# The value weights' loads moved to ScalarE's queue, and three value products moved ahead of the second tile's transposes

## The chip, the cores and the metric

One NeuronCore of a Trainium2 chip runs the whole program. The metric is the device time of one execution in microseconds; the kernel before takes 689.46 us (median of 3 runs, 689.43 to 689.73).

Five engines work side by side and each takes its own instructions in the order in which they were written: PE (TensorE, matmuls; its weight loads are shown as PEld), DVE (VectorE), ACT (ScalarE), POOL (GpSimd) and SP (SyncE, which here only issues transfers). They wait for each other, and for transfers, on semaphores.

## What is computed

A transformer layer with attention and a gated feed-forward side by side, in float32, for 2048 tokens of width 448, 16 heads of 28:

```python
xn = _layernorm(x, axis=-1)
q, k, v = xn @ wq, xn @ wk, xn @ wv            # heads of 28, 4 segments of 512 tokens
for s in range(4):
    p = softmax(qs @ ks.T * scale + mask)
    o = g * (phi(qs) @ M) / (phi(qs) @ z) + (1 - g) * (p @ vs)
    M, z = M + phi(ks).T @ vs, z + phi(ks).sum(0)
h = sigmoid(xn @ w_gate) * (xn @ w_up)
return x + o @ wo + h @ w_down
```

(Shortened from the reference; phi(t) is t+1 above zero and exp(t) below.) The change touches only the start: the normalisation of the first 512 tokens and their product with `wv`.

## The kernel before

**Precision.** Every matmul operand is split in two, a rounded high part and a low remainder, and a product is the sum of high·high, high·low and low·high. The width 448 is held in four chunks of 128 rows, the fourth holding the last 64 rows twice, so one product takes 11 matmuls. `EARLY[0]` (L52) is their order for the first two tiles: n = 0 to 2 use high parts alone (weights `wv[0..2]`), n = 3 to 5 use the low parts of x, n = 6 the fourth chunk, n = 7 to 9 the low parts of the weights (`wv[4..6]`), n = 10 the fourth chunk with `wv[7]`.

**Stages.** For each of four blocks of 512 tokens (four tiles of 128), the front normalises the rows, turns them with PE transposes, and multiplies by the value weights and then by the query/key weights (`keys_queries`, L355). Behind the front come feed-forward and attention, interleaved by a fixed plan (L785 to L794), then the output projection. PE, ACT and DVE take the front's instructions exactly as the code lists them (`FRONT`, L56); POOL's and SP's places are chosen by the scheduler.

**Start of the front (L407 to L494).** SP issues the loads. `acc[0]` receives the rows of x: tile 0 (L409), tile 1 (L410), tiles 2 and 3 in one load (L413). `raw[0]` and `raw[1]` receive the two halves of the value weights, two chunks each (L411, L412). `stage` receives four of seven query/key weight chunks in two loads (L415, L416); the rest goes to `wqk_raw` (L420, L423); `acc[1]` is the next block of x (L421); four small loads fetch the gates (L426).

Hardware transfers signal their end on eight semaphores, here called lanes 0 to 7, which the framework hands out in turn in the order in which the loads are written. A lane that comes up again is used only after its earlier load has landed: the issuing instruction waits for that.

For each tile t: `statistics` (DVE, L294 to L296), `root` (ACT, one Sqrt, L301), `normalised` (DVE reciprocal and scaling, L308 to L320; ACT copies the last 64 columns, L324), `turn_high` (four PE transposes, L95; ACT evicts the high part, L97), `turn_low` (DVE forms the low part, L102 and L103). `split_v(t)` splits chunk t of the value weights: ACT rounds it (L431), POOL subtracts (L432). `value_terms` issues the products (L335), `store_values` evicts them (ACT, L339). `fill(n)` issues n matmuls of the identity with itself whose result nobody reads; `WARM` of them (L442) stand at the very start. `gate_n` (L428) is a dummy Sqrt on ACT that brings the function table in early; the table load stands ahead of it.

Of the kernel before, what the change touches and what calls it, by code (L numbers as in the profile page):

```python
# [17 lines left out]
D = 448  # L18
# [33 lines left out]
EARLY = [HIGH + LOW_X + [(3, 3)] + LOW_W + [(3, 7)], HIGH + LOW_W + LOW_X + [(3, 3), (3, 7)]]  # L52
# [9 lines left out]
def kernel(  # L62
# [10 lines left out]
    nc = tc.nc  # L73
# [17 lines left out]
    def transpose_high(pt, src, dst, t):  # L91

        tok = slice(t * P, (t + 1) * P)
        for c in range(4):
            T.transpose(pt[:, c * P:(c + 1) * P], src[:, c * P:(c + 1) * P], ident)  # L95
        p3 = pt.rearrange("p (c n) -> p c n", c=4)
        A.activation(dst[:, 0:4, tok], p3, AF.Copy)  # L97
        return p3

    def transpose_low(p3, dst, t):  # L100
        tok = slice(t * P, (t + 1) * P)
        V.tensor_sub(dst[:, 4:7, tok], p3[:, 0:3], dst[:, 0:3, tok].bitcast(F32))  # L102
        V.tensor_sub(dst[64:, 3, tok], p3[64:, 3], dst[64:, 3, tok].bitcast(F32))  # L103
# [11 lines left out]
    def bank(name, tag):  # L115
        return ps.tile([P, L], F32, name=name, tag=tag, bufs=banks[tag])
# [32 lines left out]
    def four_k(dtype, name):  # L149
        return mid.tile([P, 2, L], dtype, name=name, tag="4k", bufs=4)  # L150
# [125 lines left out]
    with tc.tile_pool(name="front", bufs=2) as sb, tc.manual_schedule(engines=FRONT):  # L276
# [11 lines left out]
        def statistics(b, t0, steps):  # L288

            stats = sb.tile([P, steps, 6], F32, name=f"stats{steps}")  # L290
            mv = sb.tile([P, steps, 2], F32, name=f"mv{steps}")
            vh = sb.tile([P, steps], F32, name=f"vh{steps}")
            for t in range(steps):
                V.bn_stats(stats[:, t, :], acc[b][:, t0 + t, :])  # L294
                V.bn_aggr(mv[:, t, :], stats[:, t, :])
            V.tensor_scalar(vh, mv[:, :, 1], EPS, -0.5, op0=ALU.add, op1=ALU.mult)  # L296
            return mv, vh

        def root(vh):
            y = sb.tile([P, vh.shape[1]], F32, name=f"y{vh.shape[1]}")  # L300
            A.activation(y, vh, AF.Sqrt, scale=-2.0)  # L301
            return y

        def rstd(mv, vh, y):

            steps = vh.shape[1]
            tm = sb.tile([P, steps], F32, name=f"tm{steps}")
            V.reciprocal(y, y)  # L308
            if steps == 1:
                V.tensor_scalar(tm, y, y, vh, op0=ALU.mult, op1=ALU.mult)  # L310
                V.tensor_scalar(y, tm, 1.5, y, op0=ALU.add, op1=ALU.mult)
            else:
                V.tensor_mul(tm, y, y)
                V.tensor_mul(tm, tm, vh)
                V.scalar_tensor_tensor(y, tm, 1.5, y, op0=ALU.add, op1=ALU.mult)
            return [(mv[:, t, 0:1], y[:, t:t + 1]) for t in range(steps)]

        def normalise(b, t, mean, y):
            xn = sb.tile([P, 512], F32, name="xn")
            V.tensor_scalar(xn[:, :D].rearrange("p (m h c) -> p h m c", h=H, c=4),  # L320
                              acc[b][:, t, :].rearrange("p (h m c) -> p h m c", h=H, c=4), mean, y,
                              op0=ALU.subtract, op1=ALU.mult)
            if b == 0:
                A.activation(xn[:, D:], xn[:, 384:D], AF.Copy)  # L324
            else:
                G.tensor_copy(xn[:, D:], xn[:, 384:D])
            return xn
# [4 lines left out]
        def value_terms(b, t, pv, terms, n0=0, n1=len(TERMS)):  # L332
            for n in range(n0, n1):
                a, w = terms[n]
                T.matmul(pv[:, :D], xs[b][:, a, t * P:(t + 1) * P], wv[w],  # L335
                         start=n == 0, stop=n == len(TERMS) - 1)

        def store_values(b, t, pv):
            A.activation(vst[:, t, :, :DH], pv[:, :D].rearrange("p (h d) -> p h d", d=DH), AF.Copy)  # L339
            if t == NT - 1:  # L340
                nc.sync.dma_start(vd[b], vst.rearrange("p t h d -> p t (h d)"))
# [65 lines left out]
        raw = [four_k(F32, "wv_raw") for _ in range(2)]  # L407
        raw = [r.rearrange("p a n -> p (a n)")[:, :2 * D] for r in raw]
        nc.sync.dma_start(acc[0][:, 0, :], x[0:P, :])  # L409
        nc.sync.dma_start(acc[0][:, 1, :], x[P:2 * P, :])  # L410
        nc.sync.dma_start(raw[0], w_v[:, :2 * D])  # L411
        nc.sync.dma_start(raw[1], w_v[:, 2 * D:])  # L412
        nc.sync.dma_start(acc[0][:, 2:4, :], x[2 * P:L, :].rearrange("(t p) d -> p t d", p=P))  # L413
        raw = [raw[t // 2][:, t % 2 * D:(t % 2 + 1) * D] for t in range(4)]
        nc.sync.dma_start(stage[:, 0:2, :], w_qk[0:2].rearrange("c p n -> p c n"))  # L415
        nc.sync.dma_start(stage[:, 2:4, :], w_qk[2:4].rearrange("c p n -> p c n"))  # L416
        raw_qk = [stage[:, c, :] for c in range(4)]
# [8 lines left out]
                nc.sync.dma_start(gate[32 * j:32 * j + 32], beta[j::HG].partition_broadcast(32))  # L426
        G.memset(vst[:, :, :, DH:], 1.0)
        A.activation(gate_n, vst[:, 0, :NG, DH], AF.Sqrt)  # L428

        def split_v(t):  # L430
            A.activation(wv[t], raw[t], AF.Copy)  # L431
            G.tensor_sub(wv[4 + t], raw[t], wv[t].bitcast(F32))  # L432
# [10 lines left out]
        def fill(n):  # L443
            for _ in range(n):
                T.matmul(warm[:, :P], ident, ident, start=True, stop=True)

        def turn_high(t):
            p3[t] = transpose_high(bank("pt", "s"), xn[t], xs[0], t)

        def turn_low(t):  # L450
            transpose_low(p3[t], xs[0], t)

        def normalised(t):
            xn[t] = normalise(0, t, *rstd(*st[t], y[t])[0])
# [2 lines left out]
        st[0] = statistics(0, 0, 1)  # L457
        y[0] = root(st[0][1])
        normalised(0)
        st[1] = statistics(0, 1, 1)  # L460
        y[1] = root(st[1][1])
        turn_high(0)
        fill(5)
        split_v(0)
        split_v(1)
        normalised(1)
        split_v(2)
        split_v(3)
        turn_low(0)
        turn_high(1)  # L470
        st[2] = statistics(0, 2, 1)
        y[2] = root(st[2][1])
        turn_low(1)
        normalised(2)
        st[3] = statistics(0, 3, 1)
        pv = [bank("pv", "p") for _ in range(2)]
        for t in range(2):
            value_terms(0, t, pv[t], EARLY[0], 0, 7)
        value_terms(0, 0, pv[0], EARLY[0], 7)
        store_values(0, 0, pv[0])  # L480
        y[3] = root(st[3][1])
        turn_high(2)
        value_terms(0, 1, pv[1], EARLY[0], 7)
        store_values(0, 1, pv[1])
# [3 lines left out]
        pv = bank("pv", "p")  # L488
# [345 lines left out]
```

## Time and profile before

| what | value |
|---|---|
| median of 3 runs | 689.46 us |
| the profiled execution, its own time | 689.46 us |
| its span, first to last instruction | 687.7 us |
| PE busy | 681.7 us (99%) |
| DVE busy | 567.4 us (83%) |
| ACT busy | 342.6 us (50%) |
| POOL busy | 151.3 us (22%) |
| transfers | 84.37 MB, mean 123 GB/s |

A row of the timeline gives the start in us, the length, the engine, the line, the operation, what it writes and reads, how many instructions were merged, and in brackets the engine's idle time before it with what ended it. SPq is SyncE's queue; its rows are issues of transfers, not the transfers themselves. A row of the waits gives who waited, for what, us in total, how often, and the longest. A row of the transfers gives what is loaded from where, the number of issues and the size of one.

### The profile page before, as it was taken

How to read it: one execution, taken by the hardware profiler on the slowest of the kernel's cores; microseconds unless marked ns; L12 is line 12 of the kernel's file. 1: busy time of each engine (PE TensorE's matmuls, PEld its weight loads, DVE VectorE, ACT ScalarE, POOL GpSimd, SP SyncE). 2: the span in 40 equal slices, each digit the busy share in tenths (PEclk: the TensorE clock that was granted, in tenths of full speed). 3: DMA queues.
4: the chain of work that ended last, by engine and by line, in shares of the span. 5: the costliest groups of instructions: out<-in, count | busy, mean ns of one | idle time of the engine just before them, and what ended most of it. 6: DMA issues, size and time to landing. Idle time of an engine off the chain costs nothing.

```text
span 687.7 us, 10438 instructions
## 1 busy us (share of the span) xinstructions
PE 681.7 (99%) x3594; PEld 566.6 (82%) x3594; DVE 567.4 (83%) x994; ACT 342.6 (50%) x563; POOL 151.3 (22%) x349
## 2 busy tenths in 40 slices
PE   8999999999999999999999999999999999999997
PEld 7898888778878787787878878787787878878897
DVE  6765795767788988998898989989898899889863
ACT  4837555343554555543655446454653565446320
POOL 3500020101223222232332222322322322222000
PEclk9999999999999999999999999999999999999999
DMA  7446556696233323243223252314333332423342
GB/s 267 181 150 238 198 214 242 249 330 174 71 94 92 80 86 86 56 128 112 56 64 107 57 141 56 109 47 116 82 94 77 96 71 64 95 79 95 95 153 106
DMA packets 45796, 84.37 MB, mean 123 GB/s; under 512 B 6320, under 2 KB 20400, under 8 KB 45232
## 3 DMA queue, kind: packets, MB, share of 16 engines
q1 hardware_dynamic: 42736, 76.37, 35.8%
q0 software_dynamic: 3008, 7.34, 4.9%
q8 instruction: 28, 0.46, 0.3%
q14 instruction: 24, 0.20, 0.1%
HBM read 51.05 MB, written 32.64 MB: 122 GB/s over the span
## 4 chain that ended last, share of the span: by engine, by line
PE 70%; DVE 14%; issue 9%; POOL 4%; DMA 1%; ACT 1%; SPq 0%; POOLq 0%; ACTq 0%
PE pgu L247 26%; PE pd L173 13%; PE pp L355 10%; PE po L771 5%; PE pv L335 5%; PE st L612 3%; PE pa L687 3%; DVE mx L629 3%; DVE w L666 2%; POOL w L627 2%; DVE acc L174 2%; PE pmm L383 2%; PE n L401 2%; DVE hh L259 1%; DVE mx L633 1%
## 5 line engine op out<-in xcount | busy, mean ns | idle before, releaser
L247 PE MATMUL pgu<-xs,wgu 128*128 128x512 f32 x1232 | 304.1, 394 | 0.0
L247 PEld LDWEIGHTS pgu<-xs,wgu 128*128 128x128 f32 x1232 | 228.2, 188 | 47.4 <-issue 2.2
L173 PE MATMUL pd<-wdn,hh 128*128 128x448 f32 x672 | 156.0, 367 | 0.0
L627 POOL TENSOR_SCALAR_AFFINE_SELECT w<-w 128x256 f32<-128x256 f32 (+1 forms) x160 | 81.2, 509 | 236.4 <-ACT w L616 183.6
L173 PEld LDWEIGHTS pd<-wdn,hh 128*128 128x128 f32 x672 | 122.5, 188 | 12.3 <-issue 0.6
L667 ACT ACTIVATE w<-w 128x1024 f32<-128x1024 f32 (+1 forms) x96 | 87.3, 915 | 65.0 <-DVE w L666 64.2
L666 DVE TENSOR_TENSOR w<-w,mb 128x1024 f32<-128x1024 f32 (+1 forms) x96 | 98.9, 1045 | 0.1
L616 ACT ACTIVATE w<-st 128x512 f32<-128x512 f32 x128 | 74.9, 590 | 45.3 <-PE st L612 44.9
L629 DVE TRANSPOSE_TENSOR_REDUCE mx<-w 128x32 f32<-128x1024 f32 x64 | 79.0, 1235 | 17.0 <-POOL w L627 17.0
L355 PE MATMUL pp<-xs,wqk 128*128 128x512 f32 x308 | 77.7, 401 | 0.0
L174 DVE TENSOR_TENSOR acc<-pd,acc 128x448 f32<-128x448 f32 x112 | 67.1, 599 | 1.2 <-PE pd L173 1.1
L355 PEld LDWEIGHTS pp<-xs,wqk 128*128 128x128 f32 x308 | 56.8, 188 | 13.4 <-issue 2.4
L258 ACT ACTIVATE hh<-sg 128x512 fp32r<-128x512 f32 x56 | 35.2, 628 | 56.4 <-DVE sg L256 49.3
L612 PE MATMUL st<-qk 84*128 84x128 f32 (+3 forms) x256 | 61.9, 312 | 0.0
L255 ACT ACTIVATE sg<-pgu 128x512 f32<-128x512 f32 x56 | 33.2, 594 | 49.4 <-PE pgu L247 49.2
L612 PEld LDWEIGHTS st<-qk 84*128 84x128 f32 x256 | 47.6, 189 | 6.9 <-ACT w L616 0.3
L656 DVE STREAM_TRANSPOSE mb<-top 128x1024 f32<-128x1024 f32 x32 | 39.8, 1242 | 10.5 <-POOL top L653 10.1
L362 DVE TENSOR_TENSOR qk<-pp,qk 128x512 fp32r<-128x512 f32 x28 | 19.3, 688 | 29.8 <-ACT e L360 23.7
L259 DVE SCALAR_TENSOR_TENSOR hh<-sg,hh 128x512 fp32r<-128x512 f32 x56 | 38.7, 691 | 2.6 <-ACT hh L258 2.4
L335 PE MATMUL pv<-wv,xs 128*128 128x448 f32 x176 | 39.6, 376 | 0.4 <-DVE xs L102 0.3
L687 PE MATMUL pa<-w,vv 128*32 128x128 f32 (+3 forms) x512 | 39.7, 436 | 0.2
L256 DVE SCALAR_TENSOR_TENSOR sg<-sg,pgu 128x512 f32<-128x512 f32 x56 | 37.3, 665 | 1.8 <-PE pgu L247 1.6
(100 smaller groups left out, 640.6 us busy)
## 6 DMA issues: line engine op xcount, KB each, us to landing
qk<-qd SPq DMA_DIRECT2D x192, 112.0 KB
qd<-qk SPq DMA_DIRECT2D x28, 512.0 KB
raw<-in_w_ffn SPq DMA_DIRECT2D x14, 512.0 KB
vd<-vst SPq DMA_DIRECT2D x4, 1024.0 KB
vv<-vd SPq DMA_DIRECT2D x16, 256.0 KB
od<-w POOLq DMA_DIRECT2D x16, 256.0 KB, 3.8
sums<-od SPq DMA_DIRECT2D x32, 128.0 KB
out<-acc SPq DMA_DIRECT2D x16, 224.0 KB
```

What stands on the lines that cost most here:

```text
L173: T.matmul(pd[:, :D], l, r, start=n == 0, stop=n == len(mms) - 1)
L174: V.tensor_add(acc[b][:, t, :], pd[:, :D], acc[b][:, t, :])
L247: T.matmul(dst, wgu[f][:, w, side * P:(side + 1) * P], xs[b][:, a, :], start=n == 0, stop=n == len(TERMS) - 1)
L335: T.matmul(pv[:, :D], xs[b][:, a, t * P:(t + 1) * P], wv[w], start=n == 0, stop=n == len(TERMS) - 1)
L355: T.matmul(pp, wqk[c][:, w, :], xs[b][:, a, :], start=n == 0, stop=n == len(TERMS) - 1)
L612: T.matmul(st[:, at:at + L - kb * P], self.qk[:KS, 1, h, kb * P:(kb + 1) * P], self.qk[:KS, 0, h, kb * P:], start=True, stop=True)
L616: A.activation(w, st, AF.Copy)
L627: G.affine_select(d, d, pattern=pattern, base=0, channel_multiplier=-1, compare_op=ALU.is_ge, fill=MASK)
L629: V.tensor_reduce(mx[:, 16 * (n - 1):16 * (n + 1)], w3[:, n // 2, :2 * L].rearrange("p (b n) -> p b n", n=32), axis=mybir.AxisListType.X, ...
L666: V.tensor_sub(w, w, m)
L667: A.activation(w, w, AF.Exp, scale=SCALE)
L687: T.matmul(pa[32 * j:32 * j + 32, kb * P:], self.vv[:, kb, 32 * j:32 * j + 32], self.pairs[j // 2].block(j % 2, kb), start=kb == 0, stop=k ...
```

## The change

The two loads of the value weights leave SP's list and are issued by ACT, behind `gate_n`. `split_v(0)` moves ahead of tile 1's statistics, `split_v(2)` ahead of `normalised(1)`; the first three products of tile 0 (n = 0 to 2) stand ahead of tile 1's transposes, with two fills in place of five behind them; the other products of tiles 0 and 1 are spread between the later steps.

```diff
         nc.sync.dma_start(acc[0][:, 0, :], x[0:P, :])
         nc.sync.dma_start(acc[0][:, 1, :], x[P:2 * P, :])
-        nc.sync.dma_start(raw[0], w_v[:, :2 * D])
-        nc.sync.dma_start(raw[1], w_v[:, 2 * D:])
         nc.sync.dma_start(acc[0][:, 2:4, :], x[2 * P:L, :].rearrange("(t p) d -> p t d", p=P))
...
         A.activation(gate_n, vst[:, 0, :NG, DH], AF.Sqrt)
+        nc.scalar.dma_start(raw[0], w_v[:, :2 * D])
+        nc.scalar.dma_start(raw[1], w_v[:, 2 * D:])
...
         normalised(0)
+        split_v(0)
         st[1] = statistics(0, 1, 1)
         y[1] = root(st[1][1])
         turn_high(0)
-        fill(5)
-        split_v(0)
         split_v(1)
+        pv = [bank("pv", "p") for _ in range(2)]
+        split_v(2)
+        value_terms(0, 0, pv[0], EARLY[0], 0, 3)
+        fill(2)
         normalised(1)
-        split_v(2)
         split_v(3)
         turn_low(0)
         turn_high(1)
         st[2] = statistics(0, 2, 1)
         y[2] = root(st[2][1])
+        value_terms(0, 0, pv[0], EARLY[0], 3, 10)
         turn_low(1)
         normalised(2)
+        value_terms(0, 1, pv[1], EARLY[0], 0, 3)
+        value_terms(0, 0, pv[0], EARLY[0], 10)
+        store_values(0, 0, pv[0])
         st[3] = statistics(0, 3, 1)
-        pv = [bank("pv", "p") for _ in range(2)]
-        for t in range(2):
-            value_terms(0, t, pv[t], EARLY[0], 0, 7)
-        value_terms(0, 0, pv[0], EARLY[0], 7)
-        store_values(0, 0, pv[0])
         y[3] = root(st[3][1])
+        value_terms(0, 1, pv[1], EARLY[0], 3, 7)
         turn_high(2)
         value_terms(0, 1, pv[1], EARLY[0], 7)
```

How the instructions stand. First SP's queue at its start in the changed program (line numbers of the changed code; in brackets what an instruction waits for: DMAHW0 to DMAHW7 are the lanes):

```order
L409 DMA acc_69<-in_x 128x448
L410 DMA acc_69<-in_x 128x448
L411 DMA acc_69<-in_x 128x2x448
L412 DMA stage<-in_w_qk 128x2x512
L413 DMA stage<-in_w_qk 128x2x512
L417 DMA wqk_raw<-in_w_qk 128x512 x2
L418 DMA acc_70<-in_x 128x4x448
L420 DMA wqk_raw<-in_w_qk 128x512 [waits DMAHW0_49]
L423 DMA gate<-in_beta 32x4x1 [waits DMAHW2_49]
L423 DMA gate<-in_beta 32x4x1 [waits DMAHW3_49]
L423 DMA gate<-in_beta 32x4x1 [waits DMAHW5_49]
L423 DMA gate<-in_beta 32x4x1 [waits DMAHW6_49]
```

The first eight loads take lanes 0 to 7: tile 0's rows 0, tile 1's 1, tiles 2 and 3 2, the halves of stage 3 and 4, wqk_raw 5 and 6, the next block 7. The ninth, L420, is lane 0 again. Lanes 1 and 4 come up again on the two loads that are now ACT's.

ACT's start before:

```order
L428 ACTIVATE gate_n<-vst 128x4 [waits Pool_49]
L301 ACTIVATE y_171<-vh_167 128x1 [waits DVE_49]
L324 ACTIVATE xn<-xn 128x64 [waits DVE_49]
L301 ACTIVATE y_186<-vh_182 128x1 [waits DVE_49]
L97 ACTIVATE xs_65<-pt 128x4x128 [waits PE_49]
L431 ACTIVATE wv<-wv_raw 128x448 [waits DMAHW2_49]
L431 ACTIVATE wv<-wv_raw 128x448
L324 ACTIVATE xn<-xn 128x64 [waits DVE_49]
```

and in the changed program:

```order
L425 ACTIVATE gate_n<-vst 128x4 [waits Pool_49]
L426 DMA wv_raw<-in_w_v 128x896 [waits DMAHW1_49]
L427 DMA wv_raw<-in_w_v 128x896 [waits DMAHW4_49]
L301 ACTIVATE y_171<-vh_167 128x1 [waits DVE_49]
L324 ACTIVATE xn<-xn 128x64 [waits DVE_49]
L431 ACTIVATE wv<-wv_raw 128x448 [waits DMAHW1_49]
L301 ACTIVATE y_188<-vh_184 128x1 [waits DVE_49]
L97 ACTIVATE xs_65<-pt 128x4x128 [waits PE_49]
L431 ACTIVATE wv<-wv_raw 128x448
L431 ACTIVATE wv<-wv_raw 128x448 [waits DMAHW4_49]
L324 ACTIVATE xn<-xn 128x64 [waits DVE_49]
```

The two loads stand between the dummy Sqrt and tile 0's root; the first split stands ahead of the second root, the third (which waits for the second load) ahead of tile 1's copy. Further on, the splits of the query/key chunks that lie in `stage` read, in the changed program:

```order
L436 ACTIVATE wqk_116<-stage 128x512
L436 ACTIVATE wqk_117<-stage 128x512
L339 ACTIVATE vst<-pv 128x16x28 [waits PE_49]
L436 ACTIVATE wqk_118<-stage 128x512
```

`wqk_117` is the first chunk of stage's second half; before, it waited for that load's lane (DMAHW6_49), and now it has no wait of its own.

PE's start, as a difference (x4 and the like count equal instructions in a row):

```order
 L442 MATMUL warm<-ident 128x128 x10
 L95 MATMUL pt<-ident,xn 128x128 x4
-L445 MATMUL warm<-ident 128x128 x5
-L95 MATMUL pt<-ident,xn 128x128 x4
-L335 MATMUL pv<-wv,xs_65 128x448 x18
+L335 MATMUL pv<-wv,xs_65 128x448 x3
+L445 MATMUL warm<-ident 128x128 x2
+L95 MATMUL pt<-ident,xn 128x128 x4
+L335 MATMUL pv<-wv,xs_65 128x448 x15
 L95 MATMUL pt<-ident,xn 128x128 x4
```

Three of the 18 products ahead of the third tile's transposes now stand ahead of the second tile's, and two fills stand behind them where five stood before.

More of the change, by code (lines that the diff above doesn't have):

```diff
@@ L410 @@
         nc.sync.dma_start(acc[0][:, 1, :], x[P:2 * P, :])
-        nc.sync.dma_start(raw[0], w_v[:, :2 * D])
-        nc.sync.dma_start(raw[1], w_v[:, 2 * D:])
         nc.sync.dma_start(acc[0][:, 2:4, :], x[2 * P:L, :].rearrange("(t p) d -> p t d", p=P))
-        raw = [raw[t // 2][:, t % 2 * D:(t % 2 + 1) * D] for t in range(4)]
         nc.sync.dma_start(stage[:, 0:2, :], w_qk[0:2].rearrange("c p n -> p c n"))
@@ L428 @@
         A.activation(gate_n, vst[:, 0, :NG, DH], AF.Sqrt)
+        nc.scalar.dma_start(raw[0], w_v[:, :2 * D])
+        nc.scalar.dma_start(raw[1], w_v[:, 2 * D:])
+        raw = [raw[t // 2][:, t % 2 * D:(t % 2 + 1) * D] for t in range(4)]
         def split_v(t):
```

## The prediction

> **What bounds the kernel now.** I read the busy time by stretches first, then the start in order of time, then what SyncE's queue waited for.
>
> The stretches (start:end, length, then busy time and instruction count of PE, PEld, DVE, ACT, POOL; PE clock, DMA share, GB/s):
>
> ```profile
> 8.58:20.00 11.42, 11.02 (x57) 9.39 (x58) 9.02 (x27) 6.84 (x17) 6.62 (x6) 1.00 0.64 231
> 20.00:684.16 664.16, 663.95 (x3504) 550.90 (x3503) 553.53 (x953) 332.27 (x539) 142.76 (x334) 1.00 0.40 120
> ```
>
> From 20.00 to its last matmul PE idles 664.16 - 663.95 = 0.21 us. Whatever delays the first query/key products (pp, L355) delays the end by as much: nothing behind has slack to take it up. Between the second tile's transposes and 20.00 PE idles 0.40 us, so the start has little left to win. The start itself:
>
> ```profile
> 0.81 0.39 SPq L409 DMA_DIRECT2D acc<-in_x  x1
> 1.53 4.64 PE L442 MATMUL warm<-ident 128*128 128x128 f32 x20 [1.53 <-POOL ident masks.py:199]
> 2.10 0.21 ACT L428 ACTIVATE gate_n<-vst 128x4 f32<-128x4 f32 x1
> 2.19 0.43 SPq L412 DMA_DIRECT2D wv_raw<-in_w_v  x1
> 3.48 0.63 DVE L294 BATCH_NORM_STATS2 stats<-acc 128x6 f32<-128x448 f32 x1 [3.48 <-DMA acc<-in_x]
> 4.54 0.20 ACT L301 ACTIVATE y<-vh 128x1 f32<-128x1 f32 x1 [2.23 <-DVE vh L296]
> 6.10 1.01 PE L95 MATMUL pt<-ident,xn 128*128 128x128 f32 x4
> 6.95 1.28 PE L445 MATMUL warm<-ident 128*128 128x128 f32 x10
> 7.02 0.20 ACT L301 ACTIVATE y<-vh 128x1 f32<-128x1 f32 x1 [0.69 <-DVE vh L296]
> 7.15 0.60 ACT L97 ACTIVATE xs<-pt 128x512 fp32r<-128x512 f32 x1
> 7.64 1.03 ACT L431 ACTIVATE wv<-wv_raw 128x448 fp32r<-128x448 f32 x2
> 8.58 0.66 PE L95 MATMUL pt<-ident,xn 128*128 128x128 f32 x4 [0.35 <-DVE xn L320]
> 9.88 0.63 DVE L294 BATCH_NORM_STATS2 stats<-acc 128x6 f32<-128x448 f32 x1 [0.56 <-DMA acc<-in_x]
> ```
>
> Tile 0 runs as one chain: rows landed 3.48, statistics, ScalarE's root 4.54, normalised rows, transposes 6.10, eviction 7.15. VectorE also waited 0.56 us, until 9.88, for tiles 2 and 3 (L413), which stood behind the value weights. That is what moving the weights could save.
>
> **The change: its loads.** Before, every load is on SyncE's queue, and the trace shows what reusing a completion lane costs there: the ninth and later issues wait for the landing of the load that had their lane (two of them 2.0 us in all for the stage loads). So these issue times are landing times: w_v first half 7.59, second half 8.74, tiles 2 and 3 9.87, stage halves 11.22 and 12.57. L421 waited for tile 1, which had landed by 5.84.
>
> ```profile
> 5.84 0.64 SPq L421 DMA_DIRECT2D acc<-in_x  x1
> 7.59 0.53 SPq L423 DMA_DIRECT2D wqk_raw<-in_w_qk  x1
> 8.74 4.14 SPq L426 DMA_DIRECT2D gate<-in_beta  x4
> 9.87 0.31 SPq L426 DMA_DIRECT2D gate<-in_beta  x1
> 11.22 0.31 SPq L426 DMA_DIRECT2D gate<-in_beta  x1
> 12.57 0.31 SPq L426 DMA_DIRECT2D gate<-in_beta  x1
> SPq L426 <- DMA stage<-in_w_qk: 2.0, 2, 1.0
> acc<-in_x SPq DMA_DIRECT2D x3, 896.0 KB
> stage<-in_w_qk SPq DMA_DIRECT2D x2, 512.0 KB
> wv_raw<-in_w_v SPq DMA_DIRECT2D x2, 448.0 KB
> wqk_raw<-in_w_qk SPq DMA_DIRECT2D x3, 256.0 KB
> acc<-in_x SPq DMA_DIRECT2D x2, 224.0 KB
> acc<-in_x SPq DMA_DIRECT2D x1, 448.0 KB
> ```
>
> In the changed program ScalarE's first load waits on lane 1 (tile 1's rows, L410) and its second on lane 4, which is the second half of stage (L413). ScalarE takes its instructions in order, and behind that second issue stands **the root of tile 0** (L301), which has nothing to do with the weights; behind it, in turn, VectorE's reciprocal, normalised rows, PE's transposes, everything.
>
> When does stage's second half land? It landed at 12.57 with both w_v halves ahead of it; a 448 KB load costs 1.14 us in that sequence (8.74 to 9.87). The first half is issued no later than 5.84 and shares the engines, so it still comes ahead; the second, which waits, doesn't: 12.57 - 1.14 = **11.43**. Bounds: 10.29 if the first half takes nothing from SyncE's queue, 12.57 if nothing improves. I take the middle because the first half is in flight over the whole of stage's transfer.
>
> The second issue then takes about 0.43 (SyncE's own took that at 2.19), and the root begins at 11.9 where it began at 4.54: **+7.36** (bounds +6.2 and +8.5). Tile 1's and tiles 2 and 3's rows are long there, so VectorE's 0.56 us wait goes; but it is now a cover nobody needs.
>
> **The change: its order.** From root to eviction tile 0 is unchanged: transposes at 6.10 + 7.36 = 13.46, eviction 14.5 to 15.1. The first weight split (0.57) falls in ScalarE's 0.69 us idle before the second root at 7.02: nothing. The second split ends 15.7. The third needs the late load: a 224 KB load on an empty queue landed 3.48 - 0.81 = 2.67 after its issue, of which 0.57 is its bytes at the rate above; with 448 KB at half rate (2.28) that gives 11.43 + 2.10 + 2.28 = 15.8 (bounds: alone on the engines 14.7; behind all of the rest, 1664 KB, 12.57 + 4.23 = 16.8). I take 15.8, since the two queues run together. Split 15.8 to 16.4, third product 16.45. That splitting waits nowhere else: the tile 1 copy (L324) stands behind it, but PE needs the product first anyway.
>
> Now PE. It has nothing to do from 6.17 (1.53 + 4.64) to 13.46, 7.3 us. The array's rate is read here from durations, since the clock column shows 1.00 throughout the start: the 20 warm-up pieces took 232 ns each, the ten after 6.95 took 128; transposes 1.01 and 0.66. And the end of the trace:
>
> ```profile
> 684.00:685.00 1.00, 0.16 (x1) 0.00 (x0) 0.62 (x1) 0.00 (x0) 0.00 (x0) 1.00 0.11 39
> 686.20:687.70 1.50, 0.00 (x0) 0.00 (x0) 0.00 (x0) 0.00 (x0) 0.00 (x0) 0.50 0.07 26
> ```
>
> PE stops at 684.16 and from 686.20 the granted clock is 0.50. An idle of 2 us brought half rate there; 7.3 us will here. It took from 1.53 to about 6.95, 5.4 us, to come back, so I expect half rate from 13.46 to about 18.9. The Trainium skill, "TensorE: Matmul & The Clock Gate", Part 1, has half rate after an idle window of about 3.4 us and full rate after as long a busy one; by that full rate would come at about 16.9 and the sum would be about 0.6 us less.
>
> Third product 0.4, two fills (4 pieces of 0.23) 0.9: the second tile's transposes begin at 17.8, where the shifted old order had 8.58 + 7.36 = 15.94: +1.85. Against that, three products are done (L335: 16 in 3.47, 0.22 each): -0.65. The transposes at half rate: 1.01 - 0.66 = +0.35. Of PE's 0.40 us idle, 0.3 goes, since tiles 2 and 3 are early. Together **+1.25**. POOL's low splits keep ahead of the products that read them (four from 8.29 in 4.57 before; now 14.2 to about 19.3, while the last is read past 20):
>
> ```profile
> 8.29 4.57 POOL L432 TENSOR_TENSOR wv<-wv_raw,wv 128x448 fp32r<-128x448 f32 x4 [5.92 <-ACT wv L431]
> 16.52 3.47 PE L335 MATMUL pv<-wv,xs 128*128 128x448 f32 x16
> 19.83 7.67 PE L355 MATMUL pp<-xs,wqk 128*128 128x512 f32 x33
> 15.87 0.61 ACT L436 ACTIVATE wqk<-stage 128x512 fp32r<-128x512 f32 x1
> ```
>
> The number of products is unchanged; three fills fewer save nothing, they stood in idle time. The query/key weights are read from 15.87 on before and some 8 us later now, past every landing: nothing. SyncE's gate loads wait for other lanes, off the path.
>
> Sum: 7.36 + 1.25 = +8.6 on the span of 687.7: 696.3. The profiled execution took 689.46, 1.76 outside its span; it is also the median. **Forecast 698.0 us.**
>
> **Rivals.**
> 1. Same wait, but PE stays at full rate. Product and fills end at 17.2: +1.2 - 0.65 - 0.3 = +0.3, in all +7.6: 697.1. For it: warm-ups run until 6.17. Against: 684.16 to 686.20.
> 2. Same wait, and the second value load is served behind all of SyncE's rest, 16.8: third split and all behind it 1.0 later: 699.0. For it: 1664 KB are queued there first. Against: it has a queue of its own.
> 3. Not slower: the lane waits don't hold ScalarE, because the issue is handed off. Both loads leave at 2.3, half a microsecond later than SyncE's did, and land about 8 to 9. The place is the third product, ahead of the second transposes: these began at 8.58, so the split must be done by then and the load landed by 8.0. Earlier gains at most the 0.40 us of idle; at 8.3, +0.2: 689.7. For it: no load of ScalarE's is in the trace. Against: SyncE's rows wait in order, and the split of stage's second half (wqk_117) carries no wait of its own any more, so ScalarE must have waited for that landing earlier. The Trainium skill, "DMA: Bandwidth & Descriptors", section "Anatomy of one DMA", says that the DMA engines wait on no semaphore and that the issuing sequencer does so before it hands the transfer on; by that the time is the forecast's and this rival falls. SyncE's rows from 7.59 to 12.57 agree; for ScalarE nothing here shows it yet.
>
> **How the numbers follow.** Forecast 0.64, rival 1 0.12, rival 2 0.14, rival 3 0.07, something larger 0.03. The stage bounds move the forecast by 1.14 either way, 696.9 to 699.2; with rival 1 at the low bound 695.9 (6.22 + 0.3 = +6.5), with rival 2 at the high bound 700.2. So 695.8 to 700.2, leaving out rival 3 and the tail. What a measurement can tell from no change is about 0.2%, 1.4 us: rival 3 puts 0.05 inside it, 0.01 below and 0.01 above; every other case is slower: 0.94.
>
> **What would show it.** Right: ScalarE's root of tile 0 at 11 to 12.6, 0.4 to 0.5 behind the landing of stage's second half, with ScalarE idle from 4.5 on while VectorE has its statistics ready; a PE gap of about 7 us after the warm-up; transposes near 1.0 us per tile for the first two; first L355 near 28.4 (19.83 before); PE idle below 0.5 us behind it. Wrong: a root near 4.5 (rival 3), second transposes of 0.66 (rival 1), the third split later than 16.5 (rival 2). A first L355 shifted by 8.6 with an end shifted by less would refute the claim that nothing behind takes it up.

## The result, and the profile after

The changed kernel takes **700.54 us** (median of 5 runs, 699.88 to 701.74) where the kernel before takes 689.46 (5 runs beside it, 689.42 to 689.73): ratio 1.0163, 95% interval 1.0149 to 1.0177, +11.1 us. The forecast was 698.0 with 695.8 to 700.2: the sign and the lane wait are right, the size is 2.5 us short, and the median lies 0.3 above the upper bound. The profiled execution of after is the median run; its span is 698.8 (687.7 before), so the span alone grew by 11.1.

The start of the changed kernel in order of time (start, length, engine and line, operation, count, idle time before it and what ended that):

```profile
3.94 0.38 ACTq L426 DMA_DIRECT2D wv_raw<-in_w_v  x1
10.58 0.33 ACTq L427 DMA_DIRECT2D wv_raw<-in_w_v  x1
10.96 0.20 ACT L301 ACTIVATE y<-vh 128x1 f32<-128x1 f32 x1 [8.65 <-DMA wv_raw<-in_w_v]
...
12.52 1.11 PE L95 MATMUL pt<-ident,xn 128*128 128x128 f32 x4 [6.66 <-DVE xn L320]
...
18.13 0.58 ACT L431 ACTIVATE wv<-wv_raw 128x448 fp32r<-128x448 f32 x1 [3.40 <-DMA wv_raw<-in_w_v]
18.76 0.74 PE L335 MATMUL pv<-wv,xs 128*128 128x448 f32 x1 [3.23 <-ACT wv L431]
19.30 1.05 PE L445 MATMUL warm<-ident 128*128 128x128 f32 x4
20.15 1.06 PE L95 MATMUL pt<-ident,xn 128*128 128x128 f32 x4
20.86 4.00 PE L335 MATMUL pv<-wv,xs 128*128 128x448 f32 x15
...
30.96 0.39 PE L355 MATMUL pp<-xs,wqk 128*128 128x512 f32 x1
```

Two waits stand in the start that were not there before. ScalarE issues the second weight load at 10.58, and the root of tile 0 follows at 10.96 (4.54 before). PE then does two products and waits 3.23 us for the third split, until 18.76. The first query/key product comes at 30.96, 11.13 us later than before. The bracket behind the root names the load of the weights, which cannot be its cause, since the load is issued only 0.4 us ahead of it. The chain of waits of the same kernel (start, length, what) follows the issue itself back to its lane:

```profile
2.71 7.84 DMA stage<-in_w_qk
10.56 0.02 issue
10.58 7.53 DMA wv_raw<-in_w_v
```

Stage's second half lands at 10.56, 7.84 us after its issue, and lets the weight load go; this lands at 18.11, 7.53 us after its own. These two transfers are 15.4 us of the chain. The stretches of the same kernel (columns as in the prediction):

```profile
8.00:10.00 2.00, 0.00 (x0) 0.00 (x0) 0.00 (x0) 0.00 (x0) 0.00 (x0) 0.70 1.04 413
10.00:12.00 2.00, 0.00 (x0) 0.00 (x0) 0.70 (x4) 0.20 (x1) 0.00 (x0) 0.50 1.05 389
...
14.00:15.00 1.00, 0.68 (x2) 0.50 (x2) 0.93 (x4) 0.73 (x2) 0.63 (x2) 0.50 0.31 94
15.00:16.00 1.00, 0.53 (x2) 0.07 (x1) 0.94 (x3) 0.00 (x0) 0.95 (x1) 0.50 0.59 222
16.00:17.00 1.00, 0.00 (x0) 0.00 (x0) 0.73 (x3) 0.00 (x0) 0.00 (x0) 0.50 0.38 126
17.00:18.00 1.00, 0.00 (x0) 0.00 (x0) 0.00 (x0) 0.00 (x0) 0.00 (x0) 0.50 0.10 15
...
20.00:22.00 2.00, 2.00 (x9) 1.91 (x9) 0.13 (x1) 0.69 (x2) 1.01 (x1) 0.50 0.00 0
22.00:24.00 2.00, 2.00 (x10) 1.83 (x10) 1.83 (x7) 0.00 (x0) 0.00 (x0) 0.89 0.00 0
...
30.96:695.00 664.04, 663.88 (x3505) 551.06 (x3503) 553.98 (x954) 332.48 (x539) 144.48 (x334) 1.00 0.40 120
```

PE's clock is at half from 10 to beyond 22. Behind the first query/key product PE idles 664.04 - 663.88 = 0.16 us, so the delay of the start goes to the end undiminished. And from 14 to 18, for most of which PE waits for the last load, the DMA engines are between a tenth and six tenths busy. The queues' rows of the same kernel (packets, MB, share of 16 engines; q1 is SyncE's queue, q10 ScalarE's) for the stretches 3.9 to 7.8, 7.8 to 11.3, 10.6 to 14.2 and 14.2 to 18.2:

```profile
q1 hardware_dynamic: 688, 1.28, 93.8%
...
q1 hardware_dynamic: 531, 0.96, 71.9%
q10 hardware_dynamic: 144, 0.46, 32.3%
...
q1 hardware_dynamic: 850, 1.22, 95.9%
q10 hardware_dynamic: 10, 0.03, 2.3%
...
q10 hardware_dynamic: 136, 0.43, 27.5%
q1 hardware_dynamic: 428, 0.00, 5.2%
```

The first weight load, issued at 3.94, moves nothing until 7.8: all packets of the first stretch are SyncE's. In the next stretch both queues move packets. The second, issued at 10.58, moves 0.03 MB by 14.2, while SyncE's queue moves 1.22, and then needs nearly four more microseconds for 0.43 MB. Beside it SyncE's queue moves 428 packets that come to 0.00 MB: the gate loads of L423, one float a packet.

### The profile page after: what moved, and what is told of

Read it like the earlier page. It is cut to its first block, busy times and chain, and to the rows that moved or that the text cites. A ratio compares the mean times of both kernels' runs of the same rounds, so it can differ in the third digit from the quotient of the medians.

```text
span 698.8 us, 10424 instructions
## 1 busy us (share of the span) xinstructions
PE 682.9 (98%) x3588; PEld 567.6 (81%) x3588; DVE 567.6 (81%) x994; ACT 343.0 (49%) x563; POOL 152.8 (22%) x349
## 4 chain that ended last, share of the span: by engine, by line
PE 72%; DVE 12%; issue 8%; POOL 4%; DMA 2%; ACT 1%; SPq 0%; POOLq 0%; ACTq 0%
PE pgu L247 27%; PE pd L173 13%; PE pp L355 10%; PE pv L335 5%; PE po L773 5%; PE pa L689 4%; PE st L614 3%; DVE mx L631 2%; POOL w L629 2%; DVE w L668 2%; PE pmm L383 1%; PE n L401 1%; DVE acc L174 1%; DMA stage<-in_w_qk 1%; DMA wv_raw<-in_w_v 1%
## 5 line engine op out<-in xcount | busy, mean ns | idle before, releaser
L631 DVE TRANSPOSE_TENSOR_REDUCE mx<-w 128x32 f32<-128x1024 f32 x64 | 79.0, 1235 | 16.5 <-POOL w L629 16.5
L658 DVE STREAM_TRANSPOSE mb<-top 128x1024 f32<-128x1024 f32 x32 | 39.7, 1242 | 10.9 <-POOL top L655 10.5
L335 PE MATMUL pv<-wv,xs 128*128 128x448 f32 x176 | 41.3, 386 | 3.9 <-ACT wv L431 3.2
L335 PEld LDWEIGHTS pv<-wv,xs 128*128 128x128 f32 x176 | 33.5, 194 | 9.2 <-ACT wv L431 3.9
```

The costliest lines, as they stand in the source:

```text
L335: T.matmul(pv[:, :D], xs[b][:, a, t * P:(t + 1) * P], wv[w], start=n == 0, stop=n == len(TERMS) - 1)
L631: V.tensor_reduce(mx[:, 16 * (n - 1):16 * (n + 1)], w3[:, n // 2, :2 * L].rearrange("p (b n) -> p b n", n=32), axis=mybir.AxisListType.X, ...
```

## The experiments

All times are medians; the kernel before took 689.45 to 689.53 beside them. Diffs are against the changed kernel unless said.

**1. The order alone** (`order_alone`). The two loads go back to SyncE's list, in their old place; the changed order stays.

```diff
         nc.sync.dma_start(acc[0][:, 1, :], x[P:2 * P, :])
+        nc.sync.dma_start(raw[0], w_v[:, :2 * D])
+        nc.sync.dma_start(raw[1], w_v[:, 2 * D:])
...
-        nc.scalar.dma_start(raw[0], w_v[:, :2 * D])
-        nc.scalar.dma_start(raw[1], w_v[:, 2 * D:])
```

> Order of the change, loads back on SyncE where they were. Theory (ScalarE is held by the lane of stage's second half, and the late second load and half rate follow from that): root of tile 0 back at 4.5 us, third weight split about 9.3 (its half lands 8.74), second transposes about 10.8 instead of 8.6, three products and the 0.56 us idle given back: first L355 0.3 to 0.9 later than before, 689.8 to 690.4 us. Rival (the order is what costs most, by putting tile 1's copy and transposes behind the third split): over 695 us.

Measured: 690.80 (11 runs), ratio 1.0018 [1.0010, 1.0027], +1.3 us. Timeline of PE, then stretches, of this kernel:

```profile
8.69 1.67 PE L335 MATMUL pv<-wv,xs 128*128 128x448 f32 x3 [1.96 <-ACT xs L97]
11.01 1.04 PE L95 MATMUL pt<-ident,xn 128*128 128x128 f32 x4
```

```profile
7.00:8.00 1.00, 0.00 (x0) 0.00 (x0) 0.00 (x0) 0.51 (x2) 0.00 (x0) 1.00 0.97 367
8.60:10.00 1.40, 1.31 (x3) 0.95 (x4) 1.33 (x4) 1.40 (x5) 1.40 (x2) 0.50 1.04 401
```

PE idles 1.96 us between tile 0's transposes and the first product, in the place where the old order had five fills, and the clock falls to half just as the products begin. Three products take 1.67 and tile 1's transposes 1.04 (0.66 before). The time is above the 689.8 to 690.4 that was expected, which had no half rate in it; the rival is refuted.

**2. The loads alone** (`loads_alone`). ScalarE issues the loads as in the change; the order of before is kept behind them.

> Loads on ScalarE as in the change, order as before it. Theory: root of tile 0 at 10.9 us and second half landing near 18, as in the change; but tile 1's copy and transposes (about 16) no longer stand behind the third split, so only the products wait: 8.5 to 10.3 us over before, 698 to 699.8. Rival (the order costs most): under 695 us.

Measured: 697.13 (4 runs), ratio 1.0110 [1.0097, 1.0123], +7.6 us. Timeline of this kernel:

```profile
10.27 0.33 ACTq L427 DMA_DIRECT2D wv_raw<-in_w_v  x1
15.26 0.79 PE L95 MATMUL pt<-ident,xn 128*128 128x128 f32 x4
16.68 1.04 ACT L431 ACTIVATE wv<-wv_raw 128x448 fp32r<-128x448 f32 x2 [1.64 <-DMA wv_raw<-in_w_v]
17.30 3.50 PE L335 MATMUL pv<-wv,xs 128*128 128x448 f32 x16 [0.85 <-ACT wv L431]
27.11 4.27 PE L355 MATMUL pp<-xs,wqk 128*128 128x512 f32 x18
```

The root, behind the issue at 10.27, is as late as in the change. But tile 1's transposes do not stand behind the late split here: they start at 15.26, in time that PE would wait in any case. The time is below the 698 to 699.8 that was expected: the second load landed at 16.66 (10.27 + 6.39), not near 18.

**3. The change with fresh lanes** (`fresh_lanes`). The loads are written ahead of SyncE's, so that their lanes are new and nothing is waited for; the order is the change's.

```diff
+        G.memset(vst[:, :, :, DH:], 1.0)
+        A.activation(gate_n, vst[:, 0, :NG, DH], AF.Sqrt)
+        nc.scalar.dma_start(raw[0], w_v[:, :2 * D])
+        nc.scalar.dma_start(raw[1], w_v[:, 2 * D:])
         nc.sync.dma_start(acc[0][:, 0, :], x[0:P, :])
...
-        G.memset(vst[:, :, :, DH:], 1.0)
-        A.activation(gate_n, vst[:, 0, :NG, DH], AF.Sqrt)
-        nc.scalar.dma_start(raw[0], w_v[:, :2 * D])
-        nc.scalar.dma_start(raw[1], w_v[:, 2 * D:])
```

> The change with the two ScalarE loads (and the dummy Sqrt ahead of them) written ahead of SyncE's loads, so that they take lanes that no load has used; same place in ScalarE's order, behind the table load. Theory: both are issued at 2.3 to 3.1 us and the root of tile 0 is at 4.5; the 7 us go. Where the halves land tells two rivals of the queue apart: served in the order of issue over both queues, behind tiles 2 and 3 and stage, 9.0 and 11.4 us, and 692.5 us; or the two queues by turns, about 7 and 9, and 690. Rival (ScalarE's issues hold it whatever lane they have): over 695 us.

Measured: 690.12 (12 runs), ratio 1.0013 [1.0004, 1.0023]. Timeline of this kernel:

```profile
1.30 0.38 ACTq L411 DMA_DIRECT2D wv_raw<-in_w_v  x1
...
4.52 0.20 ACT L301 ACTIVATE y<-vh 128x1 f32<-128x1 f32 x1 [2.21 <-DVE vh L296]
19.84 7.69 PE L355 MATMUL pp<-xs,wqk 128*128 128x512 f32 x33
```

Both loads are still ScalarE's, on the same queue and with the same splits behind them; only the lanes and the time of issue differ. The root is back at 4.52 and 10.4 of the 11.1 us are gone. The second half landed at 8.18. Since the issues came at 1.30 and 1.72, ahead of tiles 2 and 3, and not at 2.3 to 3.1, this does not tell the two rivals of the queue apart as they were put. With no backlog ahead of the loads both queues move packets; their rows in the same kernel from 2 to 8:

```profile
q1 hardware_dynamic: 701, 1.21, 59.7%
q10 hardware_dynamic: 288, 0.92, 39.5%
```

Its runs spread from 689.41 to 692.68; the two longest have a granted clock of 0.995, the shortest of 1.00, so some half rate is still in it.

**4 and 5. Other gate loads** (`small_gates`, `small_gates_again`). The four loads of single floats become loads of 32 short rows; the gates hold other values, so the output is not the reference's.

```diff
-                nc.sync.dma_start(gate[32 * j:32 * j + 32], beta[j::HG].partition_broadcast(32))
+                nc.sync.dma_start(gate[32 * j:32 * j + 32], x[32 * j:32 * j + 32, 0:NG])
```

> The change, with the four gate loads (each 128 single floats, strided and broadcast) replaced by 32 rows of four floats of x: the gates hold other values, so the output is not the reference's; lanes and waits are unchanged. In the change the second half was issued at 10.58 and landed at 18.11, while from 14 to 18 the transfer engines were mostly idle (share 0.31, 0.59, 0.38, 0.10). Theory A (single-float gate loads issued ahead of it and beside it hold it up): it lands about 16, 2 us earlier, and the time is 1.1 to 2.5 us less, 698 to 699.4. Theory B (ScalarE's queue is slow by itself, or served behind SyncE's bytes): it lands at 17.5 to 18.5 and the time stays at 699.9 to 701.7.

> The change with the gate loads as rows of four floats, once more (the gates hold other values, so the output is not the reference's). Theory (single-float gate loads hold the second half up by 1 to 2 us): issue to landing 5 to 5.6 us as in the first such run (10.90 to 16.19). Rival (that was chance): 6 to 8.

Measured: 699.46 (4 runs), ratio 1.0144 [1.0131, 1.0157], and 699.72 (2 runs), 1.0148 [1.0128, 1.0168], against 700.54 and, beside the second, 700.71 (experiment 6): about 1 us less. The chain of waits of the first, and its ScalarE queue from 10.9 to 14.2:

```profile
10.90 5.29 DMA wv_raw<-in_w_v
```

```profile
q10 hardware_dynamic: 73, 0.26, 20.1%
```

The second load moves 0.26 MB by 14.2 where it moved 0.03; it needs 5.29 us in place of 7.53 and lands at 16.19 in place of 18.11. In the second such run it lands at 16.15, after 5.42 us. Beside the single floats it landed at 18.11, at 18.06 (experiment 6) and at 16.66 (experiment 2, in the old order), so by these profiles the floats cost it 0.5 to 1.9 us; more than 5 us from issue to landing are left without them. The first query/key product comes 2.1 us earlier in the first run (28.84) and 1.4 in the second (29.54). In the first, PE loses 1.21 us again at 177.72, in a wait for ScalarE that the changed kernel's profile does not have, and its span is only 0.7 shorter.

**6. The changed kernel again** (`again`).

> The changed kernel once more, for how far the second half's landing moves from one execution to the next: it was issued at 10.58 and landed at 18.11 (7.5 us); with the loads alone 6.4, with PE kept busy 7.0. Theory (single-float gate loads beside it): 6 to 8 us each time. Rival (the small-gates run's 5.3 is within that spread): as low as 5.3.

Measured: 700.71 (2 runs), ratio 1.0163 [1.0142, 1.0183]. Timeline of ScalarE in this execution:

```profile
11.49 0.34 ACTq L427 DMA_DIRECT2D wv_raw<-in_w_v  x1
18.09 0.58 ACT L431 ACTIVATE wv<-wv_raw 128x448 fp32r<-128x448 f32 x1 [2.44 <-DMA wv_raw<-in_w_v]
```

The second load is issued 0.9 later than in the first profile and lands 6.6 us after that, within the 6 to 8 that the theory gave; its split starts nearly where it did (18.13). In these two executions the landing did not follow the time of issue.

**7. The gate loads on another queue** (`gates_on_pool`). `nc.gpsimd` in place of `nc.sync` for the four gate loads.

> The change with the gate loads issued by POOL: nothing else moves, but the second ScalarE load now takes lane 2 (tiles 2 and 3, landed at 6.5) in place of lane 4 (stage's second half, 10.56). Root of tile 0 about 6.9 instead of 10.96. Theory (transfers of both queues are served in the order of issue, so the weights issued on ScalarE land behind all that SyncE issued before): first half still about 11.3, second half about 16, behind the seventh query/key chunk; the third split then sets the second transposes whatever the root does: 7.5 to 8.5 over before, 697 to 698. Rival (the held root sets the time, and the weights come when they are issued): the second half lands by 10, and the time is 693.5 to 696.

Measured: 702.76 (4 runs), ratio 1.0191 [1.0177, 1.0204]: slower still, and outside what either theory gave. GpSimd issues the first at 1.44, ahead of the identity matrix's last step (2.25 in place of 1.19), and the others until 4.18; SyncE's load of the next block is issued at 6.44 in place of 4.21, and tiles 2 and 3, whose lane the second weight load now waits for, land at 10.34, where 6.5 was expected. Timeline of ScalarE in this kernel:

```profile
4.54 0.38 ACTq L426 DMA_DIRECT2D wv_raw<-in_w_v  x1
16.58 0.58 ACT L431 ACTIVATE wv<-wv_raw 128x448 fp32r<-128x448 f32 x1 [4.04 <-DMA wv_raw<-in_w_v]
```

Now the first weight load needs 12 us too. The root is held until 10.74 after all. The run moves several things together, so it doesn't settle what it was made for.

**8. PE kept busy** (`warm`). The first fills grow from 10 pieces to 38 and eighteen fills stand between the second and the third product, so that PE keeps its clock through both waits.

```diff
-WARM = 10
+WARM = 38
...
-        value_terms(0, 0, pv[0], EARLY[0], 0, 3)
-        fill(2)
+        value_terms(0, 0, pv[0], EARLY[0], 0, 2)
+        fill(18)
+        value_terms(0, 0, pv[0], EARLY[0], 2, 3)
```

> The change with PE kept busy: 38 warm-ups in place of 10 and 18 fills between the second and the third product in place of two behind the third. Loads and waits unchanged. Theory (half rate costs about 1.2 of the 11.1): transposes of tile 1 take 0.66 instead of 1.06, and first L355 comes 0.8 to 1.5 earlier than in the change: 699.0 to 699.7 us, and the runs lie closer together than the change's 699.88 to 701.74. Rival (the spread and the size come from when the second half lands): time and spread as in the change.

Measured: 700.19 (4 runs, 699.46 to 701.45), ratio 1.0156 [1.0142, 1.0170]. Timeline of PE and of the third split in this kernel:

```profile
13.13 0.66 PE L95 MATMUL pt<-ident,xn 128*128 128x128 f32 x4 [0.26 <-DVE xn L320]
...
15.56 4.18 PE L445 MATMUL warm<-ident 128*128 128x128 f32 x36
18.25 0.58 ACT L431 ACTIVATE wv<-wv_raw 128x448 fp32r<-128x448 f32 x1 [3.05 <-DMA wv_raw<-in_w_v]
19.49 0.46 PE L335 MATMUL pv<-wv,xs 128*128 128x448 f32 x1
...
29.93 1.32 PE L355 MATMUL pp<-xs,wqk 128*128 128x512 f32 x5
```

The transposes run at full rate (0.66; 1.11 in after), and the first query/key product comes 1.03 earlier than in after; by the medians it is worth 0.35, less than the theory gave. But the eighteen fills are too many: the third split ends at 18.25 + 0.58 = 18.83, and the third product, which stands behind the fills, starts at 19.49, 0.66 later. So the profile bounds the worth of the lost rate (and of the two fills that gave way) by about 1.03 + 0.66 = 1.7 us of the 11. The runs spread as widely as the changed kernel's, as the rival said.

**9. The order with its fills** (`order_fills`). `order_alone` and, ahead of the three products, six fills.

```diff
+        fill(6)
         value_terms(0, 0, pv[0], EARLY[0], 0, 3)
```

> The order alone (loads on SyncE), with six fills put back behind tile 0's transposes, ahead of the three products. In the order alone PE stood idle from 6.7 to 8.7 and ran at half rate from 8.49 to 11.91 in its profile; runs spread from 689.3 to 692.02. Theory (the five fills taken out had kept PE's rate): no half rate behind 6.9, tile 1's transposes 0.66, runs within 0.6 us of each other, 689.9 to 690.3. Rival (the fills do nothing there): 690.8, spread as before.

Measured: 689.91 (11 runs, 689.38 to 690.77), ratio 1.0006 [0.9997, 1.0015]: 0.9 less than without them, as the theory gave; the spread is 1.4 us, wider than its 0.6. Timeline of PE in this kernel:

```profile
7.22 1.67 PE L445 MATMUL warm<-ident 128*128 128x128 f32 x12
10.14 0.60 PE L95 MATMUL pt<-ident,xn 128*128 128x128 f32 x4
```

**10. The second half back on SyncE** (`first_half_only`). The second half goes third in SyncE's list; ScalarE issues only the first, behind the lane of that second half.

```diff
         nc.sync.dma_start(acc[0][:, 1, :], x[P:2 * P, :])
+        nc.sync.dma_start(raw[1], w_v[:, 2 * D:])
...
         nc.scalar.dma_start(raw[0], w_v[:, :2 * D])
-        nc.scalar.dma_start(raw[1], w_v[:, 2 * D:])
```

> The change with the second half of the value weights back on SyncE, third in its order; only the first half is issued by ScalarE. It then takes lane 2, whose earlier load is that second half (landing about 6.7), so the root of tile 0 comes at about 7.1 in place of 10.96: 2.6 later than before the change, and no more. Theory A (both queues are served in the order of issue): the first half, issued at about 6.7 behind all of SyncE's loads, lands at about 16; the splits and products wait for it, 9.2 to 9.7 over before, 698.7 to 699.3 us, though the root is held 3.9 us less than in the change. Theory B (the held root sets the time, and the queues are served by turns): it lands at 9.5 to 11, 2.8 to 5.6 over before, 692.3 to 695.2 us.

Measured: 697.44 (4 runs), ratio 1.0120 [1.0103, 1.0137], +8.0 us. Timeline of this kernel:

```profile
7.01 0.37 ACTq L427 DMA_DIRECT2D wv_raw<-in_w_v  x1
7.43 0.20 ACT L301 ACTIVATE y<-vh 128x1 f32<-128x1 f32 x1 [5.12 <-DMA wv_raw<-in_w_v]
13.38 0.58 ACT L431 ACTIVATE wv<-wv_raw 128x448 fp32r<-128x448 f32 x1 [4.15 <-DMA wv_raw<-in_w_v]
14.58 1.67 PE L335 MATMUL pv<-wv,xs 128*128 128x448 f32 x3 [4.66 <-ACT xs L97]
```

The root is held 2.9 us only, and the time is still up by 8.0: the split of the first half waits for a load that took 13.35 - 7.01 = 6.3 us, and ScalarE's eviction of tile 0 stands behind that split. So a late issue can cost twice, once by holding ScalarE and once by landing late; here the landing sets the time. The 13.35 lies between strict order of issue over both queues (about 16) and turns between them (9.5 to 11); neither theory stands as it was put.

**11. Both repaired** (`best`). Fresh lanes, three fills ahead of the first products, two products there, and the third split behind tile 1's copy.

```diff
-        split_v(2)
-        value_terms(0, 0, pv[0], EARLY[0], 0, 3)
-        fill(2)
+        fill(3)
+        value_terms(0, 0, pv[0], EARLY[0], 0, 2)
         normalised(1)
+        split_v(2)
```

(With the lines of experiment 3; the next products of tile 0 begin with the third.)

> Fresh lanes for ScalarE's two loads (which landed 5.32 and 8.18 with them), three fills ahead of the first products, only two products ahead of tile 1's transposes, and the third split behind tile 1's copy. Theory: tile 1's transposes at 8.6 as before the change, two products done by then, tiles 2 and 3 at 8.2 instead of 9.9: first L355 0.3 to 0.8 earlier than before, 688.7 to 689.3 us. Rival (PE has no idle left to win, 0.40 us before): within 0.2 of before, 689.3 to 689.7.

Measured: 689.47 (11 runs, 689.41 to 689.83) beside 689.53 before, ratio 1.0000 [0.9991, 1.0009]: the rival holds. The first query/key product stands at 19.80 in its timeline, 19.83 before. That fits a start that had little left to win: behind tile 1's transposes PE idles 0.40 us before the change.

## Where the prediction was right, and the step that failed

**The bound: right.** PE idles 0.16 us behind the first query/key product; this moved by 11.13 us, the span by 11.1. The forecast said that nothing behind takes a delay up.

**The lane wait: right, and 0.9 smaller.** The step was the root of tile 0 held by lane 4, with stage's second half landing at 11.43 and the root at 11.9, +7.36. It landed at 10.56 and the root came at 10.96, +6.42, inside the bounds of 10.29 and 12.57. From the root to the transposes 12.52 - 10.96 = 1.56, as before. Experiment 3 shows the cause: with new lanes the same issues hold nothing. Rival 3, that the issue is handed off, is refuted by the root at 10.96. But the held root is not what sets the time. The sum carried +7.36 from the root to the end, with tile 0 ready for its third product just when the weights land (15.7 and 15.8). Measured, the two products ahead of it end at 14.32 + 1.21 = 15.53, and PE then waits 3.23 us for the weights: the chain of waits goes from stage's landing through the issue to the second load, without the root. The lane costs its time by issuing that load late.

**The landing of the second load: the step that failed.** I took 15.8 from two queues that share the engines, with 16.8 as the late bound ("behind all of the rest"). It landed at 18.11, later than both, though it was issued 0.9 earlier. Two things were wrong. First, it didn't share from its issue on: 0.03 MB moved in its first 3.6 us, beside 1.22 of SyncE's. The Trainium skill, "DMA: Bandwidth & Descriptors", section "Queues, rings and completion order", has each DMA engine take turns between the queues packet by packet; the rows of 7.8 to 11.3, with packets of both, agree; the rows of 3.9 to 7.8, with no packet of ScalarE's, do not, unless the load had not reached the engines by then, which no view shows. Rival 2 had the better picture, and its sign, a third split later than 16.5, is there at 18.13. Its 16.8 left out the load's own 448 KB. By the prediction's rates, SyncE's rest (4.23) and the load itself (1.14) behind stage's landing at 10.56 give 15.9, an estimate; with row loads for the gates the same sum gives 10.88 + 5.37 = 16.25, and 16.19 was measured. It is no rule: in experiment 10 a load issued at 7.01 had landed by 13.35, ahead of part of SyncE's rest. Second, "behind all of the rest" was reckoned in bytes, and the gate loads have hardly any; they cost 0.5 to 1.9 us of landing and about 1 us of the time (experiments 2 and 4 to 6). I had put them down as off the path because they wait for other lanes.

**The third product and tile 1's transposes: followed from it.** Forecast 16.45 and 17.8, measured 18.76 and 20.15: 2.3 later each. The whole miss at the first query/key product is 30.96 - 28.4 = 2.6, so 2.3 of it is there already.

**The clock: right in kind, longer.** Transposes of 1.11 and 1.06, forecast near 1.0. Half rate ended beyond 22, not at 18.9: PE idled a second time, and the rate came back some 3.7 us after it worked again at 18.76 (a mean of 0.89 in 22 to 24 puts that at about 22.4), where I had read 5.4 off the start. Fifteen products took 4.00, 0.27 each in place of 0.22. That is some 0.7 us more, and experiment 8 bounds the whole of the lost rate by about 1.7. Rival 1 falls.

**The fills: wrong, and hidden.** "Three fills fewer save nothing, they stood in idle time": they kept PE's rate. Experiments 1 and 9 price six fills in that place at 0.9 us in the order alone. In the change it could not be seen, since the long waits took the rate anyway.

**How the parts add up.** Loads alone +7.6, order alone +1.3, together 8.9; the change costs 11.1, 3.4 more than the loads alone. The two profiles show 30.96 - 27.11 = 3.85 between them. From the late split's product to the first query/key product it takes 27.11 - 17.30 = 9.8 us in the loads alone and 30.96 - 18.76 = 12.2 in the change: 2.4. Of these, 1.6 are the four fill pieces and tile 1's transposes, which the changed order puts behind the late split (19.30 to 20.86) and the old one does while the load is awaited; most of the rest is half rate. The other 1.45 are the split itself, 18.13 against 16.68. Only 0.3 of that is the later issue (10.58, 10.27); the same loads are in flight in both, and what makes up the rest was not found.

**Open:** why a load on ScalarE's queue moves nothing for some 4 us while SyncE's has work, and why single floats slow a neighbour on engines that are mostly idle. The queue rows show both; no run takes the mechanism apart. Why the loads alone landed 1.4 us earlier than the change beside the same floats is open too. A load on ScalarE's queue with SyncE's queue empty, and gate loads issued after the weights have landed, were not tried.

## What to carry to other kernels

Before a load is given to a compute engine, look up which completion lane its place in the written order gets and who holds it: whatever that engine does next waits for a transfer that it has no use for. A second queue was no sure way past a backlog here, and a load that is issued late may land later than its bytes suggest, the more so beside loads of single floats; so issue it first, or leave it where it was. Fills in idle time are worth what the clock behind them is worth: take them out only where the products that follow come at once. And a wait that grows by 7 us need not be the one that sets the time: look which of two late inputs comes last.

## What the hardware showed that I had not expected

- A load on ScalarE's queue issued at 3.94, with SyncE's loads in flight, moved its first packet after 7.8.
- From 14.2 to 18.2 ScalarE's queue moved 0.43 MB, about 108 GB/s, beside 428 packets of single floats, with the DMA engines at shares of 0.31, 0.59, 0.38 and 0.10; the stretches before had 413 and 389 GB/s from 8 to 12.
- In `order_alone` the clock fell to half within an idle of 1.96 us, and half rate stood from 8.60 to beyond 10. The Trainium skill, "TensorE: Matmul & The Clock Gate", Part 1, asks for an idle window of about 3.4 us; this run does not agree on the length of the gap.
- ScalarE's queue issued a load at 1.30 in `fresh_lanes`, while its table load, the same 1.28 us from 0.81 as before, was still running.
